# Attention and expert layers on one core: the guess of batch 2 formed ahead of its attention, units 0 and 1 summed on VectorE

## The chip, the cores and the metric

The kernel runs on one core of a Trainium2 chip. The metric is the device time of one execution in microseconds; the time of a version is the median of its runs. All times in this text are microseconds unless ns is written.

## The reference

The program takes 8 batches. Each goes through grouped-query attention (16 query heads, 4 key heads, 384 positions, head size 64), and the result, 384 tokens of width 1024 per batch, goes through a two-stage gate with 16 experts (4 groups of 4):

```python
scores = (1 / sqrt(64)) * q @ k.T            # per head, k and v repeated 4 times
attn = exp(scores - max) / sum               # softmax over the 384 keys
x = (attn @ v), heads joined -> (3072, 1024)

g_idx = argmax(x @ w_group, 1)               # one of 4 groups
e_idx = argmax(x @ w_expert[g_idx], 1)       # one of 4 experts in it
weight = softmax value of the group * softmax value of the expert
out = weight * relu(x @ w1[g, e]) @ w2[g, e]
```

## The kernel before, in words

**Attention.** A batch is worked in 24 *units*: 4 key heads by 6 blocks of 64 keys. For unit u, `score` (line 318) multiplies keys and queries on TensorE into a PSUM tile `ps_s` (two take turns), ScalarE takes the exp into a tile `e` (line 324), and `pv` (line 337) multiplies `e` by v into a tile `ps_o`. `Attn.run` issues, for each u, the scores of unit u + 2, then `pv` of unit u, then the lists of steps written for u (`steps1`, `steps2`: a step at 4.5 comes between `pv(4)` and unit 4's tail). So TensorE needs exp u twice: for `pv(u)`, and to free the score tile that unit u + 2 takes.

**Sums of the softmax.** `pair` (line 345) adds the tiles of two units on GpSimd, in place; `reduce` (line 354) sums the result over 32 columns on VectorE and keeps it in `red3`. Units listed in `apart` are not paired: VectorE reduces both tiles by themselves. `lags` says after which unit which reduction is issued. `join_keys` (line 407) adds the parts of a head; it takes one instruction for heads with equally many parts, and one a head otherwise. `sums` (line 416) adds over partitions with TensorE, and two reciprocals (line 432) write `inv`. `normalise` spreads `inv` by a transpose (line 455) and multiplies `xT` by it (line 459, on VectorE, or on GpSimd where told); `cast` (line 464) copies `xT` in bf16 to `xb`, mostly on ScalarE.

**Experts.** All tokens of a batch are first put through one expert. `moe_h` / `ffn_h` (line 636) multiplies `xb` by w1, two column blocks of 128 at a time with 8 parts of the contraction each, `ffn_y` (line 650) multiplies the result by w2, `y_out` (line 669) scales it on ScalarE and stores it. A loop at the end adds further experts where tokens need them.

**The guess.** Which expert a batch is put through is picked from the mean of v, before the attention is done: `vsum` is v summed over the blocks (three adds on GpSimd in `sum_v`, lines 112 to 114; for batch 0 one reduction on VectorE, line 121), `guess_mean` (line 480) multiplies it by a constant into two columns and copies them to `vm` (line 482), `guess_logits` (line 487) multiplies `vm` by the gate's weights, and `pick_guess` (lines 568 to 581) turns that into an index on VectorE. GpSimd reads the index (`read_pick`, line 558) and issues the loads of w1 and w2 (lines 546 and 552). From batch 3 on `pick` does the same with the logits that `gate_softmax` has.

**Order of the work.** Everything is placed by hand; each engine runs its instructions in the order written. Attention 1 (the second) runs with `steps1`, in which the first expert matmuls of batch 0 stand after unit 17. Then `first_block` finishes batch 0's experts, sums batch 1 and begins attention 2 (the third); its steps are `steps2`, with the rest of batch 1's casts, the guess for batch 2 and the gate matmuls of batch 1 (`second_gate`, line 474). `block(b)` for b from 2 on then does the experts of batch b - 1, the sums and `normalise` of batch b, its gate matmuls, and starts attention b + 1. In `block(2)` alone the guess for batch 3 is neither ahead nor left out: its mean stands between the two halves of `ffn_y` for the second row block, its logits behind the gate matmuls. GpSimd and SyncE also issue the loads: v by SyncE, k and q by GpSimd, the transposes of k and q by SyncE.

## Time and profile before

| | us |
|---|---|
| median of 3 runs (lowest, highest) | 357.18 (356.93, 357.27) |
| the profiled execution | 356.70 |
| its span, first to last instruction | 354.9 |
| TensorE busy | 345.9 |
| VectorE busy | 253.9 |
| ScalarE busy | 225.0 |
| GpSimd busy | 220.2 |

The times of single instructions come from the profiled execution, whose span is 1.8 shorter than its own time; the median is 0.48 above that time. Matmuls are pipelined, so a long duration of one says little: what counts is from one start to the next. Granted clock of TensorE over the span: 0.996 of full speed.

### The profile page before, as it was taken

How to read it: one execution, taken by the hardware profiler on the slowest of the kernel's cores; microseconds unless marked ns; L12 is line 12 of the kernel's file. 1: busy time of each engine (PE TensorE's matmuls, PEld its weight loads, DVE VectorE, ACT ScalarE, POOL GpSimd, SP SyncE). 2: the span in 40 equal slices, each digit the busy share in tenths (PEclk: the TensorE clock that was granted, in tenths of full speed). 3: DMA queues.
4: the chain of work that ended last, by engine and by line, in shares of the span. 5: the costliest groups of instructions: out<-in, count | busy, mean ns of one | idle time of the engine just before them, and what ended most of it. 6: DMA issues, size and time to landing. Idle time of an engine off the chain costs nothing.

```text
span 354.9 us, 9208 instructions
## 1 busy us (share of the span) xinstructions
PE 345.9 (97%) x3801; PEld 182.5 (51%) x3816; DVE 253.9 (72%) x520; ACT 225.0 (63%) x296; POOL 220.2 (62%) x171
## 2 busy tenths in 40 slices
PE   8999999999999999999999999999999999999994
PEld 4455565445555455554555555545545545555642
DVE  5797769767697777976689667886769677796031
ACT  5899925299536795378954499355982669444311
POOL 7889985869935499308991299804995059900000
PEclk9999999999999999999999999999999999999998
DMA  8979999799989999999999999999995995099925
GB/s 199 215 135 188 220 207 160 134 275 222 193 174 176 258 209 182 206 163 203 229 221 207 193 220 211 218 192 193 228 211 95 197 263 130 2 175 219 258 48 137
DMA packets 69327, 67.15 MB, mean 189 GB/s; under 512 B 37113, under 2 KB 49401, under 8 KB 69281
## 3 DMA queue, kind: packets, MB, share of 16 engines
q0 software_dynamic: 26640, 41.03, 67.2%
q1 hardware_dynamic: 42272, 24.94, 30.4%
q8 instruction: 32, 0.52, 0.6%
q10 hardware_dynamic: 368, 0.54, 0.4%
q14 instruction: 15, 0.11, 0.1%
HBM read 86.07 MB, written 12.58 MB: 278 GB/s over the span
## 4 chain that ended last, share of the span: by engine, by line
PE 87%; ACT 4%; POOL 3%; DVE 2%; issue 1%; DMA 1%; ACTq 0%; SPq 0%; POOLq 0%; DVEq 0%
PE ps_o L337 30%; PE ps_s L636 22%; PE ps_s L650 13%; PE ps_s L318 8%; PE ps_o L650 6%; PE ps_o L474 3%; ACT e L324 2%; POOL w L345 2%; PE ps_o L636 1%; PE ps_s L951 1%; PE ps_o L951 1%; DMA w<-in_q_dram 1%; POOL xb L466 1%; ACT w L324 0%; DVE inv L432 0%
## 5 line engine op out<-in xcount | busy, mean ns | idle before, releaser
L345 POOL TENSOR_TENSOR e<-e 128x768 f32<-128x768 f32 x91 | 162.8, 1826 | 37.0 <-PE ps_s L318 30.8
L324 ACT ACTIVATE e<-ps_s 128x768 f32<-128x768 f32 x187 | 147.7, 813 | 15.0 <-PE ps_s L318 12.8
L337 PE MATMUL ps_o<-e,v_raw 64*64 64x384 f32 x1496 | 150.1, 482 | 0.0
L354 DVE TRANSPOSE_TENSOR_REDUCE red<-e 128x24 f32<-128x768 f32 x95 | 91.4, 972 | 36.7 <-POOL e L345 36.6
L636 PE MATMUL ps_s<-xb,w 128*128 128x384 bf16 x480 | 80.1, 326 | 0.1
L337 PEld LDWEIGHTS ps_o<-e,v_raw 64*64 64x64 f32 x1496 | 55.3, 133 | 35.7 <-issue 29.5
L636 PEld LDWEIGHTS <-w 128*128 128x128 bf16 x512 | 49.4, 98 | 36.4 <-issue 4.5
L318 PE MATMUL ps_s<-qT,kT 64*64 64x384 bf16 x768 | 65.0, 325 | 0.4
L650 PEld LDWEIGHTS <-hT 128*128 128x128 bf16 x336 | 31.5, 98 | 37.7 <-issue 1.5
L650 PE MATMUL ps_s<-w,hT 128*128 128x512 bf16 x217 | 49.5, 379 | 0.4
L640 ACT ACTIVATE hT<-ps_s 128x768 bf16<-128x768 f32 x23 | 18.6, 810 | 46.7 <-PE ps_s L636 43.3
L318 PEld LDWEIGHTS <-kT 64*64 64x64 bf16 x768 | 24.5, 105 | 35.6 <-issue 33.6
L669 ACT ACTIVATE ot<-ps_s,we 128x1024 f32<-128x1024 f32 x14 | 15.6, 1115 | 19.0 <-PE ps_s L650 17.2
L604 POOL COPY tok<-qT 1x1 bf16<-1x1 bf16 x6 | 1.1, 179 | 42.5 <-DMA qT<-q_raw 42.5
L379 DVE COPY xT<-ps_o 128x768 f32<-128x768 f32 x26 | 24.0, 924 | 2.7 <-ACT xb L464 1.5
L455 DVE STREAM_TRANSPOSE e<-inv 128x768 f32<-128x768 f32 x26 | 25.2, 971 | 0.2
L464 ACT CAST xb<-xT 128x768 bf16<-128x768 f32 x28 | 23.1, 830 | 3.4 <-DVE xT L459 3.2
L650 PE MATMUL ps_o<-w,hT 128*128 128x512 bf16 x105 | 24.0, 379 | 1.1 <-issue 1.1
L459 DVE TENSOR_TENSOR xT<-xT,e 128x768 f32<-128x768 f32 x24 | 23.1, 962 | 0.8
L495 DVE STREAM_TRANSPOSE gl<-ps_o 128x96 f32<-128x96 f32 x8 | 2.3, 283 | 18.7 <-PE ps_o L474 15.0
L643 ACT ACTIVATE hT<-ps_s 128x384 bf16<-128x384 f32 x14 | 6.1, 488 | 12.5 <-PE ps_o L480 7.2
L474 PEld LDWEIGHTS ps_o<-xT,wg 128*32 128x32 f32 x448 | 9.2, 110 | 3.3 <-issue 2.1
(140 smaller groups left out, 233.3 us busy)
## 6 DMA issues: line engine op xcount, KB each, us to landing
w<-in_moe_w_dram POOLq DMA_DIRECT2D x16, 2048.0 KB, 21.9
out_dram<-ot SPq DMA_DIRECT2D x42, 256.0 KB, 6.9
q_raw<-in_q_dram POOLq DMA_DIRECT2D x7, 768.0 KB, 11.0
v_raw<-in_v_dram SPq DMA_DIRECT2D x7, 384.0 KB, 5.7
k_raw<-in_k_dram POOLq DMA_DIRECT2D x7, 192.0 KB, 6.4
out_dram<-ot SPq DMA_DIRECT2D x10, 128.0 KB, 2.4
w<-in_q_dram POOLq DMA_DIRECT2D x3, 192.0 KB, 6.3
w<-in_k_dram SPq DMA_DIRECT2D x2, 192.0 KB, 3.7
```

Source lines behind the costliest of these rows:

```text
L318: nc.tensor.matmul(out=sT[r * H2:(r + 1) * H2, s, :S], lhsT=kT[b][s * D:(s + 1) * D, key_block(b, s, g // 2, c), ks], rhs=qT[b][s * D:(s + ...
L324: nc.scalar.activation(e.rearrange("p t (s x) -> p s t x", s=2), sT[:, :, :S].rearrange("p s (t x) -> p s t x", t=2), ACT.Exp, scale=scale)
L337: nc.tensor.matmul(out=oT[t * D:(t + 1) * D, r, :S], lhsT=vraw[b][r * H2:(r + 1) * H2, g // 2, c * D:(c + 1) * D], rhs=self.e[u][r * H2:(r ...
L345: nc.gpsimd.tensor_add(out=self.e[u - 1], in0=self.e[u - 1], in1=self.e[u])
L354: nc.vector.tensor_reduce(out=red3[b][:, g, parts[b][g]].rearrange("p t j -> p (t j)"), in_=self.e[w].rearrange("p t (j x) -> p (t j) x", ...
L379: nc.vector.tensor_copy(out=dst, in_=src)
L455: nc.vector.transpose(out=rb.rearrange("p k (j x) -> p k j x", x=32), in_=inv[b][:, ks].unsqueeze(3).to_broadcast([P, 2, NB, 32]))
L459: eng.tensor_mul(out=x, in0=x, in1=rb)
L464: nc.scalar.copy(out=xb[b][:, ks, :], in_=xT[b][:, ks, :])
L474: nc.tensor.matmul(out=pt[32 * t:32 * t + 32, 0, :S // 4], lhsT=wg[:, head_pair(m), :], rhs=x[:, t], start=(m == 0), stop=(m == KQ - 1))
L636: nc.tensor.matmul(out=h[:, jj, :S], lhsT=w1[:, head_pair(m), (f0 + jj) * P:(f0 + jj + 1) * P], rhs=x[:, m, :], start=(m == 0), stop=(m == ...
L650: nc.tensor.matmul(out=y[:, nh, :], lhsT=hT[:, f, c * P:(c + 1) * P], rhs=w2[:, f, nh * HALF:(nh + 1) * HALF], start=(f == 0), stop=(f == ...
```

## The change

- The v of batch 2 is summed by one reduction on VectorE in the steps after unit 17 of the second attention, not by three adds on GpSimd in `first_block`.
- The product for the guess of batch 2 stands behind the sums of batch 1 in `first_block`, in columns 192 and 193 of the same PSUM tile, and `vm` is copied behind the reciprocals. The logits and the pick stand after unit 1 of the third attention (before: the mean after unit 1, logits and pick after unit 2).
- In the third attention units 0 and 1 are not paired on GpSimd: VectorE reduces both after unit 2. Head 0 then has four parts and the others three, so head 0 is joined apart, after unit 10.
- The three casts of batch 1 that stood after units 1, 3 and 6 stand together at 4.5, behind the gate matmuls.
- In `block(2)` the mean of the guess for batch 3 comes behind the gate matmuls, and its logits behind the first scores of attention 3.
- `ffn_h` with f0 = 0 (in every batch) takes the first 6 parts of the contraction for both column blocks, then the last 2 parts.

```diff
--- before.py
+++ after.py
@@ -115,12 +115,12 @@
                              in1=s[:, :, 2 * D:])
         vsum[b] = t
 
-    def first_sum_v():
-        vsum[0] = gpool.tile([P, NA * D], BF16, name="vsum")
+    def reduce_v(b):
+        vsum[b] = gpool.tile([P, NA * D], BF16, name="vsum")
         with nc.allow_low_precision(reason="the guess of an expert alone reads this"):
             nc.vector.tensor_reduce(
-                out=vsum[0].rearrange("p (a d) -> p a d", d=D),
-                in_=vraw[0].rearrange("p a (c d) -> p a d c", d=D), axis=AX.X, op=ALU.add)
+                out=vsum[b].rearrange("p (a d) -> p a d", d=D),
+                in_=vraw[b].rearrange("p a (c d) -> p a d c", d=D), axis=AX.X, op=ALU.add)
 
     def new_qT(b):
         qT[b] = xpool.tile([P, KQ * SC, P], BF16, name="qT")
@@ -409,8 +409,9 @@
                 in_=red3[b][:, g:h, :parts[b][g]].rearrange("p g c t j -> p g (t j) c"),
                 axis=AX.X, op=ALU.add)
 
-    def sums(b, g0, g1, which, tiles=False):
-        sm = ps_tile(which)[:, :, :(g1 - g0) * 2 * NB]
+    def sums(b, g0, g1, which, tiles=False, mean=None):
+        pt = ps_tile(which)
+        sm = pt[:, :, :(g1 - g0) * 2 * NB]
         for r in range(2):
             if not tiles:
                 nc.tensor.matmul(out=sm[:, r], lhsT=half32[:, r, :],
@@ -423,6 +424,8 @@
                     out=sm[t * D:(t + 1) * D, r].rearrange("p (g t j) -> p g t j", t=2, j=NB)[:, :, t],
                     lhsT=half32[rs, r, t * D:(t + 1) * D], rhs=red[b][rs, g0:g1, t],
                     start=True, stop=True)
+        if mean is not None:
+            guess_product(mean, pt, MEAN)
         if b not in inv:
             inv[b] = gpool.tile([P, KQ, NB], F32, name="inv", bufs=2)
         iv = inv[b][:, 2 * g0:2 * g1].rearrange("p (g r) j -> p r g j", r=2)
@@ -430,6 +433,7 @@
         for t in range(2):
             ts = slice(t * D, (t + 1) * D)
             nc.vector.reciprocal(out=iv[ts], in_=sm[ts, :, :, t])
+        return pt if mean is None else guess_copy(pt, MEAN)
 
     Q = P // 4
 
@@ -475,12 +479,19 @@
                                  lhsT=wg[:, head_pair(m), :], rhs=x[:, t],
                                  start=(m == 0), stop=(m == KQ - 1))
 
+    MEAN = 2 * KQ * NB
+
+    def guess_product(b, pt, n):
+        nc.tensor.matmul(out=pt[:, 1, n:n + 2], lhsT=vsum[b], rhs=halfb, start=True, stop=True)
+
+    def guess_copy(pt, n):
+        vm = gpool.tile([P, 2], BF16, name="vm")
+        nc.vector.tensor_copy(out=vm, in_=pt[:, 1, n:n + 2])
+        return vm
+
     def guess_mean(b, pt):
-        pm = pt[:, 1, :2]
-        nc.tensor.matmul(out=pm, lhsT=vsum[b], rhs=halfb, start=True, stop=True)
-        vm = gpool.tile([P, 2], BF16, name="vm")
-        nc.vector.tensor_copy(out=vm, in_=pm)
-        return vm
+        guess_product(b, pt, 0)
+        return guess_copy(pt, 0)
 
     def guess_logits(vm, out_):
         for r in range(2):
@@ -631,11 +642,13 @@
 
     def ffn_h(x, w1, hT, f0, which):
         h = ps_tile(which)
-        for jj in range(2):
-            for m in range(KQ):
-                nc.tensor.matmul(out=h[:, jj, :S],
-                                 lhsT=w1[:, head_pair(m), (f0 + jj) * P:(f0 + jj + 1) * P],
-                                 rhs=x[:, m, :], start=(m == 0), stop=(m == KQ - 1))
+        ends = [0, KQ] if f0 else [0, KQ - 2, KQ]
+        for m0, m1 in zip(ends, ends[1:]):
+            for jj in range(2):
+                for m in range(m0, m1):
+                    nc.tensor.matmul(out=h[:, jj, :S],
+                                     lhsT=w1[:, head_pair(m), (f0 + jj) * P:(f0 + jj + 1) * P],
+                                     rhs=x[:, m, :], start=(m == 0), stop=(m == KQ - 1))
         if f0 + 2 < FQ:
             nc.scalar.activation(hT[:, f0:f0 + 2, :], h[:, :, :S], ACT.Relu)
         else:
@@ -730,7 +743,7 @@
     index_constants()
     steps0 = {
         0: [gate_matrix_2],
-        2: [do(first_q1, "x"), first_sum_v],
+        2: [do(first_q1, "x"), do(reduce_v, 0)],
         4: [do(first_k, NC, 2 * NC, "x")],
         7: [do(x_mean, 0)],
         8: [do(x_logits, 0)],
@@ -780,6 +793,7 @@
             lambda: mean(1, state["pt"]),
             do(at[1].pair, 7),
             do(at[1].reduce, 7),
+            do(reduce_v, 2),
             do(moe_h, 0, 2, "s"),
             do(at[1].pair, 13),
             do(at[1].pair, 15),
@@ -799,13 +813,12 @@
     def first_block():
         load_v(3)
         moe_y(0, 0, "s")
-        sum_v(2)
         load_k(3)
         load_q(3)
         at[1].reduce(NU - 1)
         join_keys(1, 0, Hkv)
         y = ffn_y(w2s[0], hTs[0], 1, "s", (0,))
-        sums(1, 0, Hkv, "o")
+        state["vm"] = sums(1, 0, Hkv, "o", mean=2)
         ffn_y(w2s[0], hTs[0], 1, "s", (1,), y)
         y_out(0, 1, y)
         y = ps_tile("o")
@@ -813,7 +826,7 @@
         normalise(1, 2, "x")
         cast(1, 0)
         ffn_y(w2s[0], hTs[0], 2, "o", (0,), y)
-        at[2] = Attn(2, later=(1,), lags={5: [1], 6: [3], **{u: [u - 2] for u in range(7, NU, 2)}})
+        at[2] = Attn(2, apart=(1,), lags={6: [3], **{u: [u - 2] for u in range(7, NU, 2)}})
         at[2].score(0)
         at[2].score(1)
         ffn_y(w2s[0], hTs[0], 2, "o", (1,), y)
@@ -821,6 +834,10 @@
         normalise(1, 1, None, pool)
         normalise(1, 3, None, pool)
 
+    def second_logits():
+        state["pt"] = ps_tile("x")
+        x_logits(2)
+
     def second_gate():
         gate_logits(1, state["pt"])
         state["gl"] = gate_rows(state["pt"], False)
@@ -828,12 +845,11 @@
     first_block()
     before_attention(2)
     steps2 = {
-        1: [do(cast, 1, 2), do(at[2].pair, 1), do(x_mean, 2)],
-        2: [do(x_logits, 2)],
-        3: [do(cast, 1, 1)],
-        4.5: [second_gate],
-        6: [do(cast, 1, 3)],
+        1: [second_logits],
+        2: [do(at[2].reduce, 1)],
+        4.5: [second_gate, do(cast, 1, 2), do(cast, 1, 1), do(cast, 1, 3)],
         8: [do(read_pick, 2)],
+        10: [do(join_keys, 2, 0, 1)],
     }
     at[2].run(steps2)
 
@@ -865,7 +881,7 @@
             pick_w2(b)
         moe_h(f, 0, "s")
         at[b].reduce(NU - 1)
-        join_keys(b, 0, Hkv)
+        join_keys(b, int(b == 2), Hkv)
         if b == 2:
             gate_softmax(1, state["gl"], False)()
             out_weights(1)
@@ -893,16 +909,16 @@
         y = ffn_y(w2s[f], hTs[f], 1, "s", (0,))
         if ahead:
             guess_logits(vm, guess_out(pt))
-        elif not last:
-            vm = guess_mean(b + 1, pt)
         ffn_y(w2s[f], hTs[f], 1, "s", (1,), y)
         y_out(f, 1, y)
         gate_logits(b, pt)
         if not (last or ahead):
-            guess_logits(vm, guess_out(pt))
+            vm = guess_mean(b + 1, pt)
         if b <= EARLY:
             at[b + 1] = Attn(b + 1)
             at[b + 1].start()
+        if not (last or ahead):
+            guess_logits(vm, guess_out(pt))
         cast(b, 3)
         w = gate_softmax(b, gate_rows(pt, not last), not last)
         if not last:
```

Three engines show how the order moves. First ScalarE, from the second exp of the third attention on (`e` are the exps, `ot` the output scaling of batch 0's third row block, `xb` the casts of batch 1). Before:

```order
L324 ACTIVATE e<-ps_s_1158 128x2x2x192
L669 ACTIVATE ot<-ps_o_1134,we 128x1024
L324 ACTIVATE e<-ps_s_1188 128x2x2x192
L324 ACTIVATE e<-ps_s_1200 128x2x2x192
L464 CAST xb<-xT 128x768
L324 ACTIVATE e<-ps_s_1217 128x2x2x192
L324 ACTIVATE e<-ps_s_1243 128x2x2x192
L464 CAST xb<-xT 128x768
L324 ACTIVATE e<-ps_s_1256 128x2x2x192
L324 ACTIVATE e<-ps_s_1301 128x2x2x192
```

and with the change:

```order
L324 ACTIVATE e<-ps_s_1158 128x2x2x192
L682 ACTIVATE ot<-ps_o_1134,we 128x1024
L324 ACTIVATE e<-ps_s_1188 128x2x2x192
L324 ACTIVATE e<-ps_s_1200 128x2x2x192
L324 ACTIVATE e<-ps_s_1227 128x2x2x192
L324 ACTIVATE e<-ps_s_1241 128x2x2x192
L324 ACTIVATE e<-ps_s_1253 128x2x2x192
L468 CAST xb<-xT 128x768 x3
L324 ACTIVATE e<-ps_s_1301 128x2x2x192
```

The casts that stood behind exps 3, 5 and 8 now stand in a row behind exp 6.

Next GpSimd in `first_block`, from the weight loads of batch 1's expert on. Before:

```order
L552 DMA w_1068<-in_moe_w_dram 128x8x1024
L112 TENSOR_TENSOR vs<-v_raw 128x384
L113 TENSOR_TENSOR vs<-vs 128x2x64
L114 TENSOR_TENSOR vsum<-vs 128x128
L96 DMA k_raw<-in_k_dram 128x2x384
L101 DMA q_raw<-in_q_dram 128x8x384
L459 TENSOR_TENSOR xT<-xT,e 128x768 x2
```

and with the change:

```order
L563 DMA w_1070<-in_moe_w_dram 128x8x1024
L96 DMA k_raw<-in_k_dram 128x2x384
L101 DMA q_raw<-in_q_dram 128x8x384
L463 TENSOR_TENSOR xT<-xT,e 128x768 x2
L345 TENSOR_TENSOR e<-e 128x768 x3
```

The three adds on v are gone, so the loads of k and q of batch 3 follow the weights at once; behind the two multiplies come eleven pair sums (three and eight) where there were twelve.

Last VectorE, from the joins of batch 1 into the third attention. Before:

```order
L407 TENSOR_REDUCE red<-red_842 128x24 x4
L432 RECIPROCAL inv<-ps_o_1116 64x2x4x12 x2
L455 STREAM_TRANSPOSE ps_o_1136<-inv 128x2x384
L459 TENSOR_TENSOR xT<-xT,ps_o_1136 128x768
L455 STREAM_TRANSPOSE ps_o_1139<-inv 128x2x384
L459 TENSOR_TENSOR xT<-xT,ps_o_1139 128x768
L455 STREAM_TRANSPOSE e<-inv 128x768 x2
L482 CAST vm<-ps_o_1213 128x2
L568 TENSOR_REDUCE km<-ps_o_1213 128x1
```

and with the change:

```order
L407 TENSOR_REDUCE red<-red_842 128x24 x4
L435 RECIPROCAL inv<-ps_o_1113 64x2x4x12 x2
L489 CAST vm<-ps_o_1113 128x2
L459 STREAM_TRANSPOSE ps_o_1136<-inv 128x2x384
L463 TENSOR_TENSOR xT<-xT,ps_o_1136 128x768
L459 STREAM_TRANSPOSE ps_o_1139<-inv 128x2x384
L463 TENSOR_TENSOR xT<-xT,ps_o_1139 128x768
L459 STREAM_TRANSPOSE e<-inv 128x768 x2
L579 TENSOR_REDUCE km<-ps_o_1211 128x1
```

The copy of `vm` moved from behind the last transposes up to behind the reciprocals. Further down the two reductions of units 0 and 1 come behind the pick and ahead of the transpose of the gate's logits:

```order
L592 TENSOR_SCALAR oh_all<-ps_o_1211 128x16
L354 TENSOR_REDUCE red_1238<-e 128x24 x2
L506 STREAM_TRANSPOSE gl<-ps_o_1211 128x96
L379 COPY xT<-ps_o_1195 128x768
L354 TENSOR_REDUCE red_1238<-e 128x24 x3
L407 TENSOR_REDUCE red<-red_1238 128x24
L354 TENSOR_REDUCE red_1238<-e 128x24
```

Before, one reduction stood behind that transpose in place of the two ahead of it, and there was no join of one head:

```order
L581 TENSOR_SCALAR oh_all<-ps_o_1213 128x16
L495 STREAM_TRANSPOSE gl<-ps_o_1213 128x96
L354 TENSOR_REDUCE red_1313<-e 128x24
L379 COPY xT<-ps_o_1195 128x768
L354 TENSOR_REDUCE red_1313<-e 128x24 x4
```

## Rows read from the trace of the kernel before

**Rows 1.** The page, part 4: the chain that ended last, share of the span by engine.
```profile
PE 87%; ACT 4%; POOL 3%; DVE 2%; issue 1%; DMA 1%; ACTq 0%; SPq 0%; POOLq 0%; DVEq 0%
```

**Rows 2.** Timeline of TensorE, 43.2 to 47 us: start us, us, engine, line, operation, tiles, count.
```profile
44.29 3.01 PE L636 MATMUL ps_s<-xb,w 128*128 128x384 bf16 x16
```

**Rows 3.** Chain of waits, 30 to 100 us: start us, us, what.
```profile
44.66 0.82 POOL xb L466
...
45.52 1.78 PE ps_s L636 x10
...
66.90 0.43 PE ps_o L416 x4
...
68.11 0.77 DVE inv L432
...
77.95 0.16 DVE oh_all L581
```

**Rows 4.** Timeline of TensorE, 72.9 to 83.5 us (the third attention).
```profile
78.16 1.53 PE L474 MATMUL ps_o<-xT,wg 128*32 128x96 f32 x64
79.61 0.36 PE L318 MATMUL ps_s<-qT,kT 64*64 64x384 bf16 x4
...
82.06 0.33 PE L318 MATMUL ps_s<-qT,kT 64*64 64x384 bf16 x4
...
83.12 0.36 PE L318 MATMUL ps_s<-qT,kT 64*64 64x384 bf16 x4
```

**Rows 5.** Timeline of GpSimd, 60 to 100 us.
```profile
66.94 0.45 POOL L113 TENSOR_TENSOR vs<-vs 128x128 f32<-128x128 f32 x1
...
77.43 21.41 POOL L345 TENSOR_TENSOR e<-e 128x768 f32<-128x768 f32 x12
```

**Rows 6.** Timeline of all engines, 95.2 to 101 us (block 2).
```profile
95.04 5.37 PE L636 MATMUL ps_s<-xb,w 128*128 128x384 bf16 x32
...
99.89 0.48 DVE L407 TENSOR_REDUCE red<-red 128x96 f32<-128x288 f32 x1
...
100.94 0.33 PE L636 MATMUL ps_s<-xb,w 128*128 128x384 bf16 x1
```

**Rows 7.** Chain of waits, 95 to 118 us.
```profile
101.11 5.20 PE ps_s L636 x32
...
113.24 1.46 PE ps_o L474 x64
...
115.29 0.16 issue
```

**Rows 8.** Line 121: engine, operation, tiles, count: ns min/median/max, first and last start us.
```profile
L121 DVE TENSOR_REDUCE vsum<-v_raw x1: 1519/1519/1519, 11.3 to 11.3; 128x128 bf16<-128x768 f32 x1
```

**Rows 9.** Timeline of VectorE, 48.5 to 51.8 us (idle before, and who ended it).
```profile
48.91 0.16 DVE L482 CAST vm<-ps_o 128x2 bf16<-128x2 f32 x1 [1.73 <-PE ps_o L480]
48.99 0.97 DVE L354 TRANSPOSE_TENSOR_REDUCE red<-e 128x24 f32<-128x768 f32 x1
51.57 0.28 DVE L495 STREAM_TRANSPOSE gl<-ps_o 128x96 f32<-128x96 f32 x1 [1.62 <-PE ps_o L487]
```

**Rows 10.** Timeline of ScalarE, 68 to 84 us.
```profile
73.09 1.11 ACT L669 ACTIVATE ot<-ps_o,we 128x1024 f32<-128x1024 f32 x1
74.10 1.50 ACT L324 ACTIVATE e<-ps_s 128x768 f32<-128x768 f32 x2
75.48 0.84 ACT L464 CAST xb<-xT 128x768 bf16<-128x768 f32 x1
76.20 1.53 ACT L324 ACTIVATE e<-ps_s 128x768 f32<-128x768 f32 x2
```

**Rows 11.** Timeline of VectorE, 105 to 113 us (block 2).
```profile
112.63 0.16 DVE L482 CAST vm<-ps_o 128x2 bf16<-128x2 f32 x1
```

**Rows 12.** Timeline of VectorE, 66.6 to 73.1 us (after the second attention).
```profile
67.35 1.52 DVE L432 RECIPROCAL inv<-ps_o 64x96 f32<-64x96 f32 x2 [1.64 <-PE ps_o L416]
```

**Rows 13.** Timeline of GpSimd, 106 to 110 us (block 2).
```profile
107.89 1.26 POOL L113 TENSOR_TENSOR vs<-vs 128x128 f32<-128x128 f32 x1
```

## The prediction

> **What bounds the kernel now.** I read the page's chain of waits first: 87% of it is TensorE [rows 1], so the time is the length of TensorE's queue plus the places where that queue stands still. A wait between other engines that TensorE does not share costs nothing. From the end of the third attention (95.1 us) on I found one stall of TensorE in the chain; the others lie between 44 and 83 us. So I read the chain for 30 to 100 us and the timelines of single engines there.
>
> The reader should see four places. (1) The first expert matmuls of batch 0 (line 636) begin at 44.29 [rows 2]. Six of the sixteen run; the other ten start only at 45.52, when GpSimd's last cast ends at 45.48 [rows 3]. (2) In the third attention a unit costs TensorE 0.82 us where nothing waits: three of them from 79.61 to 82.06 [rows 4]. Unit 9 comes 1.06 after unit 8 (83.12), behind an exp that stood behind a cast on ScalarE. (3) The gate matmuls of batch 1 (line 474) start at 78.16, and the last operation of the guess on VectorE ended at 78.11 [rows 3, 4]: they wait for the guess. (4) GpSimd's twelve pair sums run without a gap from 77.43 to 98.84 [rows 5]. The join behind them ends at 100.37, and TensorE, done with 32 matmuls from 95.04, needs that join for the sums of batch 2 [rows 6].
>
> **The change part by part.** Times are on the old clock of the profiled execution.
>
> *First expert matmuls, split 6 and 2 (ffn_h with f0 = 0).* Thirty-two such matmuls take 5.20 us [rows 7], so 0.1625 each. Six from 44.29 end at 45.27; the seventh starts at 45.52. With the change twelve come ahead of the part that needs the cast and end at 46.24, after the cast. The stall of 45.52 - 45.27 = 0.25, taken as **-0.24**, goes. The split adds no instruction; in the later blocks the casts are done long before, and it changes nothing.
>
> *Sum of v for batch 2 on VectorE.* One reduction: the same form ran once, in 1519 ns [rows 8]. It enters behind the reduction that ends at 49.96, in an idle stretch of 1.62 us that ends at 51.57 with TensorE's matmuls for the guess [rows 9]. It ends at 51.48; those matmuls come 0.24 earlier than before, so VectorE's gate chain starts 0.1 earlier than before instead of 0.24. The sums of batch 1 that hang on that chain have more room than this (third rival). So **0**, hidden. GpSimd's three adds go, and the loads of k and q of batch 3 are issued some 2 us earlier, behind the same two weight loads in the same queue; I give that nothing.
>
> *Product for the guess beside the sums of batch 1, cast of vm behind the reciprocals.* The product is a matmul more here and one less in the attention. The cast of 0.16 lies in the chain of reciprocals, transpose, multiply and ScalarE's first cast, ahead of the output scaling at 73.09 [rows 10]. Two rows bound it. Behind a vm cast at 48.91 the next instruction began at 48.99, before the cast had ended: 0.08 [rows 9]. The second reciprocal, which moves from partitions 0-63 to 64-127, began at 68.11 and took 0.77 [rows 3], half of the 1.52 that both took from 67.35 [rows 12]: no overlap. The vm cast comes behind that second one and goes back to partition 0, so I take the whole 0.16; the ends are 0 and 0.2. The Trainium skill, VectorE: DVE Perf Modes, section Two Vector instructions with no wait between them, has this as a rule: an instruction that starts in another quadrant of partitions than the last one on that memory is held until all before it have finished. With the row at 48.91 the total below would be -1.22, by the rule it is -1.14.
>
> *The third attention.* On ScalarE two exps back to back take 1.38 (74.10 to 75.48), so 0.69 each, a cast 0.72 (75.48 to 76.20), the output scaling 1.01 (73.09 to 74.10) [rows 10]; an exp's result is there 0.81 after its start. Now three casts stand together behind exp 6. ScalarE with the 0.16: scaling 73.25, exp 2 at 74.26, exps 3 to 6 at 74.95, 75.64, 76.33 and 77.06 (0.04 allowed for TensorE's scores), casts 77.75, 78.47, 79.19, exp 7 at 79.91, ready at 80.72. TensorE: unit 2 waits for exp 2 (ready 75.07) and starts at 75.12, with the guess's two matmuls hidden in that wait; units 3 and 4 at 75.94 and 76.76; the gate matmuls at 77.68 instead of 78.16, since the guess on VectorE now starts a unit earlier and is done by about 77.0. They last 1.45 (78.16 to 79.61 [rows 4]): unit 5 at 79.13, unit 6 at 79.95, unit 7 at 80.77 (exp 7 and TensorE itself arrive within 0.05 of each other), unit 8 at 81.59, unit 9 at 82.41. Before, it was 83.12 [rows 4]: **-0.71**. From there the exps (0.69) outrun the units (0.82), as before. The ends: -0.88 if the vm cast is free and no exp is late, -0.4 if each of the six steps to exp 7 takes 0.05 more.
>
> *Units 0 and 1 summed by VectorE; first group joined apart.* GpSimd loses one sum of 21.41 / 12 = 1.78 [rows 5]. VectorE gains one reduction (0.97 [rows 9]) and a small join, in a stage where it often waits for GpSimd. GpSimd's last sum then ends near 97.1 and the join near 98.6, 1.8 earlier. TensorE's 32 matmuls from 95.04 end at 100.24, the sums take 0.43 where nothing waits (66.90 [rows 3]), so the next matmul should come at 100.67; it came at 100.94 [rows 6]. That wait, **-0.27**, goes. (If GpSimd were not relieved, the 0.95 gained before would all be lost here.) What is late next is VectorE's work up to the gate of batch 2 (first rival).
>
> *Guess for batch 3 moved behind the gate matmuls.* No instruction more; its logits now stand between eight score matmuls and line 650. Nothing in the old trace shows that order. The nearest row is the 0.16 of issue between those scores and line 650 [rows 7]. I take **+0.08**, half of one more such gap; the ends are -0.05 and +0.3 (two gaps). VectorE's gate chain there starts some 0.6 later, and only the next pick and a late output wait for it.
>
> Sum: -0.24 - 0.71 - 0.27 + 0.08 = **-1.14**. The profiled execution took 356.70 (span 354.9), 0.48 under the median of the three runs, so it would take 355.6, and the median is 357.18 - 1.14 = **356.0**. With all ends on the good side it is -1.44 (355.7), on the bad side -0.6 (356.6).
>
> **The rivals.**
>
> *Taken back at the gate of batch 2.* If VectorE's chain after the join does not move, the gate matmuls there cannot start before its last multiply, which ended by 112.63 [rows 11]; they started at 113.24 [rows 7]. Then at most 0.61 of the gain survives: 357.18 - 0.61 + 0.08 = 356.65. For it: the chain is serial, from the join through a softmax, reciprocals and four multiplies. Against: it starts 1.8 earlier when GpSimd does. Chance 0.16.
>
> *The three casts cost what they save.* Three casts in a row are 2.16 of ScalarE; the gate matmuls cover 1.45. If exp 7 comes 0.7 later than I worked out (a cast waiting for GpSimd's multiply, for instance), unit 9 is where it was, and only 0.24 + 0.27 - 0.08 = 0.43 is left: 356.75. For it: exp 7 and TensorE meet within 0.05. Against: GpSimd's multiplies for those casts are done when its pair sums begin, 77.43 [rows 5], before the first cast. Chance 0.13.
>
> *Slower: the new reduction on VectorE is stretched beside GpSimd.* It stands ahead of VectorE's gate chain, which ends in the pick that GpSimd reads ahead of its last four pair sums; behind these come the last reduction, the joins, and the sums of batch 1 at 66.90. A short add of GpSimd shows what stretching can do: 0.45 at 66.94 [rows 5], 1.26 at 107.89 [rows 13], a factor of 2.8. The joins were done 1.64 before the reciprocals at 67.35, at 65.71 [rows 12], and TensorE would come to the sums near 66.6, so it decides from about 0.9 us over 1.52. At 2.8 times 1.52 = 4.25 TensorE would wait 1.85, and the time is 357.18 - 1.14 + 1.85 = 357.9. Against: the 1519 ns [rows 8] are the whole instruction in a stage where GpSimd was summing pairs too. Chance 0.06. The Trainium skill, GPSIMD Engine Reference, section 8 Key points, puts such contention on VectorE instructions with two inputs in SBUF or in a two-port mode; the reduction has one input, and the 1.26 stood beside a multiply with two.
>
> **How the numbers follow.** The forecast has 0.65, the rivals 0.16, 0.13 and 0.06. About 0.2% (0.7 us) is what a measurement of this kernel can tell from no change, so faster means below 356.47. Of the forecast some 0.62 lies there; its bad end and the first two rivals (356.6 to 356.8) are no change, 0.31; the third rival and a little unknown are slower, 0.07. The range holds the forecast's ends and the first two rivals: 355.5 to 356.9.
>
> **What would show it.** In the new profile: no gap after the sixth expert matmul at 45; the reduction of line 121 near 50 lasting 1.5; gate matmuls of batch 1 less than 0.2 after unit 4's end; three casts in a row on ScalarE and unit 7 without a wait over 0.1; eleven pair sums in a row on GpSimd; no wait of the sums of batch 2 for the join. It is wrong if TensorE waits in the third attention as long as before, if the gate of batch 2 waits for VectorE, or if the sums of batch 1 wait for the joins.

## The result, and the profile after

The changed kernel takes **360.31 us** (median of 8 runs, 359.00 to 362.65) where the kernel before takes 357.33 (8 runs, 356.93 to 358.47): ratio 1.0083, 95% interval 1.0054 to 1.0112. It is slower by 3.0 us; the forecast was 356.0, and the range ended at 356.9. The profiled execution took 360.43 (span 358.7).

Up to 135 us nearly everything came as forecast. These rows answer to the four places of the prediction. First the chain of waits of the changed kernel, 30 to 125 us (start us, us, what):

```profile
44.39 2.71 PE ps_s L649 x16
...
67.91 0.76 DVE inv L435
...
68.69 0.17 DVE vm L489
...
68.88 1.00 DVE ps_o L459
...
77.51 1.46 PE ps_o L478 x64
...
99.64 0.42 PE ps_o L417 x4
100.05 5.20 PE ps_s L649 x32
```

The sixteen expert matmuls from 44.39 run in one piece; before, they broke after six [rows 2, 3]. The cast of vm stands whole in the chain at 68.69: the reciprocal ahead of it ends at 68.67, the transpose behind it starts at 68.88, so the cast costs its 0.17 and a little more. The gate matmuls of batch 1 start at 77.51 by this view, where they started at 78.16 [rows 4]. In block 2 the sums are followed at once by the next matmul (99.64 + 0.42 = 100.06); the 0.27 of [rows 6] is gone. VectorE and TensorE by their timelines:

```profile
49.86 1.46 DVE L121 TENSOR_REDUCE vsum<-v_raw 128x128 bf16<-128x768 f32 x1
51.36 0.28 DVE L506 STREAM_TRANSPOSE gl<-ps_o 128x96 f32<-128x96 f32 x1
```

```profile
77.44 1.53 PE L478 MATMUL ps_o<-xT,wg 128*32 128x96 f32 x64
...
79.73 0.33 PE L318 MATMUL ps_s<-qT,kT 64*64 64x384 bf16 x4
...
80.73 0.36 PE L318 MATMUL ps_s<-qT,kT 64*64 64x384 bf16 x4
...
82.35 0.36 PE L318 MATMUL ps_s<-qT,kT 64*64 64x384 bf16 x4
```

and ScalarE, 70 to 84 us (exps 2 to 6, the three casts, exp 7 and on):

```profile
74.03 3.76 ACT L324 ACTIVATE e<-ps_s 128x768 f32<-128x768 f32 x5
77.68 2.29 ACT L468 CAST xb<-xT 128x768 bf16<-128x768 f32 x3
79.87 4.56 ACT L324 ACTIVATE e<-ps_s 128x768 f32<-128x768 f32 x6
```

The reduction for vsum took 1.46 us, not stretched. Unit 9 of the third attention starts at 82.35, where it started at 83.12 [rows 4]. Unit 7 comes at 80.73, next to the 80.77 that I had worked out, but that nearness is luck: 80.77 was on the old clock, without the 0.24 of the split, and with it unit 7 should have come at 80.53. It is 0.20 late, 1.00 behind unit 6 where a unit costs 0.82, so the sign "unit 7 without a wait over 0.1" is not met. ScalarE's exps 2 to 6 took 3.65 (74.03 to 77.68) where I had given them 3.49; with the casts, exp 7 began 0.20 late.

The simplest way to see where time goes is to lay the two traces side by side and follow the start of the same matmul in both, after minus before:

| place | shift, us | step |
|---|---|---|
| behind the first expert matmuls, 47 us | -0.21 | -0.24 |
| unit 9 of the third attention, 83 us | -0.78 | -0.58 |
| behind the sums of batch 2, 101 us | -1.05 | -0.27 |
| first unit of the fourth attention, 119 us | -1.06 | 0 |
| behind the guess product of block 3, 148 us | +2.10 | **+3.15** |
| 24 matmuls later, 154 us | +3.78 | **+1.69** |
| end | +3.78 | 0 |

So the sum of my terms, -1.14, was there as -1.06, and then 4.84 us are lost in one place, in block 3, where the diff changes nothing. The chain of waits of the changed kernel there, 136 to 160 us:

```profile
136.72 2.14 POOL e L345 x2
138.86 7.38 DMA qT<-q_raw
...
146.81 0.89 POOL q_raw L101
...
147.71 1.02 POOL vs L112
...
148.81 1.06 POOL vs L113
...
149.94 0.47 POOL vsum L114
...
150.45 0.18 PE ps_o L485
150.63 6.89 PE ps_s L663 x24
```

and the waits in the same stretch, first of the changed kernel, then of the kernel before (engine, line, waited for: us in total, times, longest):

```profile
POOL q_raw L101 <- DMA qT<-q_raw: 5.0, 1, 5.0
...
PE ps_o L485 <- POOL vsum L114: 3.0, 1, 3.0
...
POOL k_raw L96 <- DMA kT<-k_raw: 0.8, 1, 0.8
```

```profile
POOL q_raw L101 <- DMA qT<-q_raw: 1.5, 1, 1.5
```

GpSimd and TensorE in the kernel before, by their timelines:

```profile
143.54 0.89 POOL L101 DMA_DIRECT2D q_raw<-in_q_dram  x1 [1.50 <-DMA qT<-q_raw]
144.45 1.01 POOL L112 TENSOR_TENSOR vs<-v_raw 128x384 f32<-128x384 f32 x1
145.54 0.47 POOL L113 TENSOR_TENSOR vs<-vs 128x128 f32<-128x128 f32 x1
146.09 0.47 POOL L114 TENSOR_TENSOR vsum<-vs 128x128 bf16<-128x128 f32 x1
```

```profile
148.37 0.17 PE L480 MATMUL ps_o<-halfb,vsum 128*128 128x2 bf16 x1
```

To be read from the bottom: TensorE's product for the guess of batch 4 (line 485, one small matmul) waits 3.0 us for GpSimd's vsum. GpSimd forms it with three adds (147.71 to 150.41), which stand in its queue behind the loads of k(5) and q(5). Load_q may not overwrite q_raw before the DMA transposes of q(4) have read it, and these were issued at 138.86 and landed 7.38 us later; GpSimd waited 5.0 us for them, before 1.5. In the kernel before vsum was there at 146.56 and TensorE came at 148.4: 1.8 us to spare, so nothing showed. Now TensorE comes 1.06 earlier and vsum 3.85 later.

The last row of the chain holds the other 1.69: 24 matmuls took 6.89 us, 5.21 before (148.53 to 153.74). The window table of the changed kernel gives the granted clock (window, its length, busy time and count of PE, PEld, DVE, ACT and POOL, then PEclk, DMA share, GB/s):

```profile
147.40:150.50 3.10, 0.12 (x3) 0.05 (x3) 2.12 (x2) 2.42 (x4) 2.82 (x4) 1.00 0.87 178
150.50:157.60 7.10, 7.10 (x28) 2.90 (x29) 3.85 (x5) 1.77 (x2) 0.00 (x0) 0.76 1.31 150
```

TensorE worked 0.12 of the 3.10 us of waiting, and got a mean clock of 0.76 in the 7.1 us behind it; 151.5 to 153.0 us shows 0.50, the lower level of 1.2 GHz. On the page the slice of PEclk there is an 8 between slices of 9.

Why is vsum 3.85 later? 0.58 of it is GpSimd's second add (line 113), which took 1.06 here and 0.47 before; no run shows why. The other 3.27 is load_q, issued at 146.81 instead of 143.54. The loads form a chain of their own on GpSimd and the DMA queues: transposes of q(3) land, a small copy on GpSimd that waits for them (tok, line 615) lets the weight loads of batch 2 go, behind these k and q of batch 4 are loaded, then transposed, then load_q(5) may go, then the sum. This chain does not contain TensorE, so it did not get shorter by 1.06. It got longer, at two places: the transposes of q(3) took 7.2 us instead of 5.5, those of q(4) 7.4 instead of 5.6. The DMA views around the former, first of the kernel before, then of the changed kernel:

```profile
qT<-q_raw SPq DMA_TRANSPOSE x1, 5.5
```

```profile
q8 instruction: 1, 0.02, 0.8%
q14 instruction: 1, 0.01, 0.2%
...
qT<-q_raw SPq DMA_TRANSPOSE x1, 7.2
```

### The profile page after: what moved, and what is told of

Same layout as the page of the kernel before. It is cut to its first block, busy times and chain, and to the rows that moved or that the text cites. A ratio compares the mean times of both kernels' runs of the same rounds, so it can differ in the third digit from the quotient of the medians.

```text
span 358.7 us, 9221 instructions
## 1 busy us (share of the span) xinstructions
PE 348.5 (97%) x3816; PEld 183.3 (51%) x3816; DVE 257.2 (72%) x523; ACT 225.0 (63%) x296; POOL 216.3 (60%) x167
## 4 chain that ended last, share of the span: by engine, by line
PE 89%; DMA 3%; ACT 3%; POOL 2%; DVE 1%; issue 1%; ACTq 0%; SPq 0%; POOLq 0%; DVEq 0%
PE ps_o L337 33%; PE ps_s L649 19%; PE ps_s L663 14%; PE ps_s L318 9%; PE ps_o L663 6%; PE ps_o L478 3%; DMA qT<-q_raw 2%; ACT e L324 2%; PE ps_o L649 1%; PE ps_s L967 1%; PE ps_o L967 1%; DMA w<-in_q_dram 1%; POOL e L345 1%; ACT w L324 0%; DVE inv L435 0%
## 5 line engine op out<-in xcount | busy, mean ns | idle before, releaser
L345 POOL TENSOR_TENSOR e<-e 128x768 f32<-128x768 f32 x90 | 161.0, 1826 | 34.8 <-PE ps_s L318 31.4
L354 DVE TRANSPOSE_TENSOR_REDUCE red<-e 128x24 f32<-128x768 f32 x96 | 92.4, 972 | 36.0 <-POOL e L345 35.7
L663 PE MATMUL ps_s<-w,hT 128*128 128x512 bf16 x224 | 51.5, 388 | 0.0
L663 PE MATMUL ps_o<-w,hT 128*128 128x512 bf16 x112 | 25.5, 380 | 0.0
L463 DVE TENSOR_TENSOR xT<-xT,e 128x768 f32<-128x768 f32 x24 | 24.2, 1008 | 0.8
```

The lines of the kernel that those rows point to most:

```text
L345: nc.gpsimd.tensor_add(out=self.e[u - 1], in0=self.e[u - 1], in1=self.e[u])
L354: nc.vector.tensor_reduce(out=red3[b][:, g, parts[b][g]].rearrange("p t j -> p (t j)"), in_=self.e[w].rearrange("p t (j x) -> p (t j) x", ...
L463: eng.tensor_mul(out=x, in0=x, in1=rb)
L663: nc.tensor.matmul(out=y[:, nh, :], lhsT=hT[:, f, c * P:(c + 1) * P], rhs=w2[:, f, nh * HALF:(nh + 1) * HALF], start=(f == 0), stop=(f == ...
```

## The experiments

Theory 1: the change gains its 1.06 us, and the loss is TensorE's wait for GpSimd's sum in block 3 with the slow clock behind it. Theory 2: some part of the change costs the time by itself. Theory 3: the late transposes cost it whatever stands behind them. With a time I give the ratio to the kernel before, run beside it, and the 95% interval. A caution for single traces: some profiled executions, one of the changed kernel too, are up to 1 us late within the first 20 us already; I take shifts from behind that point.

### Where the sum stands, and the parts alone

The sum ahead of the loads, in the changed kernel (e1) and in the kernel before (e2):

```diff
+            if not last:
+                sum_v(b + 1)
             if b + 2 < B:
                 load_k(b + 2)
                 load_q(b + 2)
-            if not last:
-                sum_v(b + 1)
```

> The changed kernel with one more edit: in the blocks from batch 3 on, GpSimd forms the tile sum for the next guess before it issues the loads of k and q, not behind them. Theory 1 (the loss is TensorE's wait for GpSimd's vsum in block 3, because that sum stands behind load_q, which waits until the transposes of q have read q_raw): vsum is there at about 143 us, TensorE arrives at 147.4 and waits for nothing, the 3.0 us of wait and the 1.7 us of slow clock behind it go, and the gain of 1.06 us that the trace shows up to 135 us reaches the end: 356.2 us, 1.1 under the kernel before. The transposes of q may still take 7.2 us. Theory 2 (a part of the change costs the time itself, by more traffic or a slower clock): the time stays at 360. Theory 3 (late transposes are the cause whatever stands behind them: the loads of the later batches come late too): the wait moves to the next user of these loads and 358 to 360 us are left.

Measured: 358.60 us (12 runs, 357.16 to 363.46), ratio 1.0030 (1.0005 to 1.0055). The wait for vsum and the slow clock are gone and TensorE keeps 1.06 us up to 180 us, as theory 1 says. But it does not reach the end, and the time is in the range of theory 3, though the transposes of q(4) took 5.51 here: in blocks 4 and 5 of the profiled run it loses 0.63, 0.65 and 0.68 at matmuls that start at 191.28, 223.51 and 234.62, each right behind the landing of a weight load (191.23, 223.46, 234.58). The waits there, of which the one put down to ScalarE is the third of these:

```profile
PE ps_s L649 <- DMA w<-in_moe_w_dram: 0.6, 1, 0.6
PE ps_s L663 <- ACT hT L656: 0.5, 1, 0.5
PE ps_s L663 <- DMA w<-in_moe_w_dram: 0.5, 1, 0.5
```

> The kernel before with the same move of GpSimd's sum ahead of the loads from batch 3 on, nothing else. Theory 1: no wait is there to be taken away (vsum is ready at 146.6 us, TensorE comes at about 148.5), so the time stays within 0.3 us of 357.3. Theory 2 says nothing else. Theory 3: loads of k(5) and q(5) are issued up to 1.8 us later, so up to +0.5 us if a later guess hangs on them.

Measured: 358.25 (12 runs), 1.0039 (1.0023 to 1.0054): slower, which theory 1 in its simple form had not said. In its trace the load of k(5) is asked for at 144.0 instead of 141.3 us, since the sum stands ahead. The profiled run (358.23) keeps step with the kernel before up to 245 us and then loses 0.95, in the seventh attention and block 6. There the transposes of q(7) land at 247.45 instead of 240.34, GpSimd stands at the copy that waits for them, its pair sums begin at 249.85 instead of 246.11, and TensorE waits for copies of outputs behind them. So even the kernel before cannot have its loads 2 us later for nothing; theory 3 has a part in it.

Next the parts alone: the split of ffn_h on the kernel before (e3), and the changed kernel with ffn_h in one pass (e4):

```diff
+        ends = [0, KQ] if f0 else [0, KQ - 2, KQ]
+        for m0, m1 in zip(ends, ends[1:]):
```

> The kernel before with only the first pair of ffn_h of each batch split in two passes over its depth. Theory 1: TensorE runs 0.2 us ahead, which leaves 1.7 us of the 1.9 us that vsum is early in block 3, so the 0.2 us reach the end: 357.1 us, unless the transposes of q of batches 3 and 4 take 7.2 us in place of 5.5, in which case vsum is 1.5 to 3 us later and part of a wait is back. Theory 2 (the split itself costs, for it is in every batch): slower than 357.3 by 0.5 us or more, the same in each batch.

Measured: 357.46, ratio 1.0001 (0.9991 to 1.0011). That is not the 357.1 of theory 1, and no cost of the split either. In its profiled run, the slowest of the 12 (358.74), the 0.24 us are there up to block 3; the transposes of q(4) took 7.06, vsum came at the moment at which TensorE did (0.08 lost), and TensorE then waited for the weights of batch 3 at 180 and 191 us (+0.92 and +0.61). The gain of the split does not reach the end.

> The changed kernel with ffn_h in one pass as before; the guess, the pair summed on VectorE and the first group joined apart all stay. Theory 1: TensorE is 0.85 us ahead in block 3; with transposes of q of 5.5 us nothing waits and it takes 356.5 us, with two of 7.2 us it waits 2.8 us and then loses 1.7 to the clock: 360. So the time must go with the wait of that product for vsum in its own trace. Theory 2 (guess part costs the time): 360.3 and no such wait in block 3.

Measured: 360.84 (359.19 to 361.48), 1.0090 (1.0071 to 1.0110). Transposes of q(3) and q(4) of 7.2 and 7.3 us, a step of +2.79 at the product in block 3 and +1.46 behind it: theory 1's second case.

### The changed kernel once more

> The changed kernel once more, for a second profile. Theory 1: the same wait of TensorE for vsum in block 3, 2.5 to 3.5 us, with a granted clock under 1 behind it, and the transposes of q of batches 3 and 4 at 7.1 to 7.4 us each. If it is chance that they were slow, one of them takes 5.5 us here, and the wait is shorter by 1.6 us.

Measured: one run, 363.11 us. Both transposes slow again (7.18 and 7.53), the step at the product 0.55 larger than in the first profile, and that behind it 2.75 instead of 1.69: after the wait 22 matmuls took 7.28 us. The start of this run was 1.0 late. These three make up the 2.6 us between the two profiles; the other runs of the changed kernel have no trace.

### Giving the chain room, one place at a time

E5 fetches the weights of batch 3 ahead of the loads of batch 5 (in block 3: sum, copy, weights, load_k, load_q). `EARLY` is the first block that loads k and q ahead of the weights:

```diff
         if not early:
+            if b > 2:
+                sum_v(b + 1)
             after_transposes(b + 1)
             pick_w1(b)
             pick_w2(b)
-            sum_v(b + 1)
+            if b == 2:
+                sum_v(b + 1)
             load_k(b + 2)
             load_q(b + 2)
...
-    EARLY = 3
+    EARLY = 4
```

> The changed kernel, in whose block 3 GpSimd now forms the tile sum first and then fetches the weights of batch 3 ahead of the loads of k and q of batch 5 (as block 2 does for its own; one block more is treated that way, so the first two units of the fifth attention's successor are scored in block 4 too). Theory 1 with a second bound, which the run with the sum moved first gave (1.05 us ahead up to 180 us, then three waits of 0.63, 0.65 and 0.68 us for weights that land late): the weights of batch 3 land about 12 us earlier, at 176 us against a need at 179 us, so neither the wait for vsum nor those of block 4 are there, and the gain of 1.06 us reaches the end: 356.3 us. If the loads of batch 5, which then come behind the weights, are late in turn, a wait appears for the weights of batch 4 at 222 or 233 us: up to 358. Theory 2 (a part of the change costs the time by itself): 358 to 360.

Measured: 357.33 (12 runs, 355.76 to 360.43), 1.0014 (0.9988 to 1.0039). In the profiled run, at 355.76, TensorE waits for no other engine between 60 and 350 us and ends 0.83 ahead of the kernel before. Half the runs lie between 355.8 and 356.6, half between 358.1 and 360.4: right in the one, the "late in turn" of the expectation fits the other, whose traces I do not have.

E6 and e7 leave out the copy of block 2, in the changed kernel and in the one before:

```diff
         if not early:
-            after_transposes(b + 1)
             pick_w1(b)
```

> The changed kernel without the small copy on GpSimd in block 2 that makes the weight loads of batch 2 wait until the transposes of q of batch 3 have landed; the sum for the guess stays behind load_q in block 3. Theory 1 (the chain transposes, weights, k and q, transposes, load_q, sum sets when vsum is there): the weights are asked for some 10 us earlier, k and q of batch 4 land at about 128 us, their transposes are done before GpSimd comes to load_q at 141 us, vsum is ready at about 144 us against TensorE's 147.4, no wait, 356.3 us. If weights and transposes slow each other, the transposes of batch 3 land later, but nothing needs them before 118 us. Theory 2: 360.

> The kernel before without that same copy in block 2. Theory 1: no wait to take away, 357.3 us within 0.3; if it gets faster by more, the kernel before had waits for these loads in its usual runs that its one trace does not show.

Measured: 371.58, 1.0399 (1.0386 to 1.0413), and 357.90, 1.0015 (1.0007 to 1.0024). The transposes of q(3) took 28.6 us beside the weight loads in the first and 9.5 in the second. "Nothing needs them before 118 us" was wrong: the scores of the next attention do, at 113.7, and TensorE waited 13.1 us for them. E7, for which 357.3 within 0.3 was expected, is a miss too: it is slower, not equal. That copy has to stay in block 2.

E9 puts the sum between the two loads, e10 a second copy ahead of them in block 3:

```diff
             if b + 2 < B:
                 load_k(b + 2)
+            if not last:
+                sum_v(b + 1)
+            if b + 2 < B:
                 load_q(b + 2)
-            if not last:
-                sum_v(b + 1)
```

```diff
+            if b == EARLY:
+                after_transposes(b + 1)
             if b + 2 < B:
                 load_k(b + 2)
```

> The changed kernel with GpSimd's sum between the loads of k and q in the blocks from batch 3 on, so that the load of k(5) is again asked for at 141.1 us, some 2.2 us into the transposes of q(4). Theory 1: vsum is ready at about 143.7 us and no wait for it is left. Theory on the transposes (those of q(4) land 1.7 us late where the load of k(5) is asked for 2.0 to 2.2 us into them, as in three traces, and not where it comes 3.4 us into them or later, as in the traces with the sum first): they take 7.2 us or more here, so load_q comes at about 146.8 and the weights of batch 3 land as in the changed kernel, at 181.2 and 193.2 us, against needs of 179.4 and 189.8: waits of about 1.8 and 1.6 us in block 4 in the place of the one taken away, 359.5 us. If the place of that load does not matter, the transposes take 5.5 us and the time is that with the sum first, 358.6.

Measured: 360.84, 1.0097 (1.0074 to 1.0120). The transposes of q(4) took 7.31 as expected and no wait for vsum was left; but those of q(5) took 7.18 too, and the loss appeared at a place I had not named, in the fifth attention:

```profile
POOL tok L615 <- DMA qT<-q_raw: 17.8, 1, 17.8
DVE red L354 <- POOL e L345: 10.4, 4, 8.0
...
PE ps_o L337 <- DVE xT L379: 3.7, 1, 3.7
```

GpSimd stood at the copy that waits for q(5) until 166.2 us, so its pair sums of the fifth attention began at 168.6; VectorE's reduction waited 8.0 us for the first of them, the copy of an output to SBUF (line 379) stood behind that reduction, and TensorE waited 3.7 us for the copy.

> The changed kernel with its own order on GpSimd (load of k, load of q, sum) in block 3, but the three held until the transposes of q(4) have landed. Theory on the transposes: without the load of k(5) in them they take 5.5 us and land at 144.4 us instead of 146.2; load_q is asked for at 145.2, vsum is ready at 148.8 instead of 150.4, so TensorE waits 1.4 us instead of 3.0 and loses less to the clock behind it: 358 to 359 us, faster than the changed kernel though a wait was added. If that load has nothing to do with it, the transposes take 7.2 us still, vsum comes at 150.7 and the time is 360.5 or more.

Measured: 361.46 (359.55 to 362.88), 1.0117 (1.0088 to 1.0146). Right on the transposes, 5.51 us; wrong on the time. The held loads were issued at 145.95 and 146.69, and the three adds took 3.5 us instead of 2.7, so vsum came at 151.1 and TensorE waited 3.2 us, as long as in the changed kernel. The run is worth having for the clock behind that wait:

```profile
147.80:151.20 3.40, 0.23 (x4) 0.06 (x3) 2.40 (x3) 2.42 (x4) 3.12 (x3) 1.00 1.10 191
151.20:156.60 5.40, 5.40 (x28) 2.47 (x29) 3.85 (x5) 1.77 (x2) 0.00 (x0) 1.00 1.29 144
```

The 24 matmuls took 5.20 us here (a step of +3.34 and none behind it), against 6.89. About the same idle time (2.98 and 3.17 us) cost 1.7 us of clock in one run and nothing in the other.

E11 is e1 with the copy left out in block 3; e12 and e13 are that again, with the first scores of batch 5 moved into block 4, on the changed kernel and on the kernel before:

```diff
                 before_attention(b + 1)
-                after_transposes(b + 2)
+                if b > EARLY:
+                    after_transposes(b + 2)
```

and, in e12 and e13 alone:

```diff
-        if b <= EARLY:
+        if b <= EARLY + 1:
             at[b + 1] = Attn(b + 1)
...
-            elif b + 1 < B:
+            elif EARLY + 1 < b < B - 1:
                 nxt = at[b + 1] = Attn(b + 1)
```

> The changed kernel with the sum ahead of the loads from batch 3 on, and in block 3 alone without the copy that makes the weight loads of batch 3 wait for the transposes of q(5). Theory 1 with the second bound: the weights of batch 3 are asked for at about 146 us, behind the loads of k and q of batch 5 in the queue, and land at about 172 and 184 us, before TensorE needs them at 179.4 and 189.8; the transposes of q(5), which then run beside them, take 20 us and more, but nothing needs them before about 184 us. No wait in blocks 3 and 4: 356.3 us. If those transposes land after 186 us, the loads of batch 6 on GpSimd and with them the weights of batch 4 come late, and a wait at 222 or 233 us takes the gain back: 357 to 359.

Measured: 362.60, 1.0157 (1.0139 to 1.0175). Weights early, as expected; the transposes of q(5) took 26.8 us, and "nothing needs them before about 184 us" was wrong, since the fifth attention ends with scores of the sixth, which need q(5):

```profile
PE ps_s L318 <- DMA qT<-q_raw: 5.0, 1, 5.0
```

> The changed kernel with the sum ahead of the loads, without the copy in block 3 that holds the weights of batch 3 behind the transposes of q(5), and with the first two units of the fifth batch's attention scored in block 4 and not at the end of the attention before it, so that these transposes, which take some 27 us beside the weights, have until about 199 us. Theory 1 (the change itself is worth what the forecast said, and only GpSimd's chain of loads took it back): no wait for vsum, for the weights of batch 3 (there at 169 and 181 us against 179.4 and 189.8), for those transposes (183 us) or for GpSimd's pair sums; the gain of 1.06 us reaches the end but for what the later scores cost, 0 to 0.5 us: 356.2 to 356.8, and 0.8 to 1.2 us under the same edits on the kernel before. Theory 2 (the change costs the time by itself): 358 to 360 and slower than the same edits on the kernel before.

> The same edits on the kernel before. Theory 1: nothing waited there, so 357.3 us plus what the later scores cost, 0 to 0.5 us: 357.3 to 357.8, and 0.8 to 1.2 us over the run above.

Measured: 359.70, 1.0080 (1.0052 to 1.0108), and 357.93, 1.0019 (1.0005 to 1.0033). From 116 us on the first profile is 1.16 ahead of the second, and stays so up to 230 us: nothing waits in blocks 3 and 4. Then the weights of batch 4 are late (0.54) and in the seventh attention a copy of an output behind GpSimd's late pair sums (1.17). By their times alone these two runs are what theory 2 had said, 358 to 360 and slower than the same edits on the kernel before; the traces show a lead that lasts past the change and is lost at the loads of later blocks. The chain had been given room in one block and taken it from the next.

E14 and e15 are e1 with the loads of v moved, to see whether these make the links long:

```diff
-        if b + 2 < B:
+        if b + 2 < B and not early:
             load_v(b + 2)
...
                 before_attention(b + 1)
+                load_v(b + 2)
                 after_transposes(b + 2)
```

and in e15, which has no load of v at the head of block 2 either:

```diff
         moe_y(f, 0, "s")
+        if not early:
+            load_v(b + 2)
```

> The changed kernel with the sum ahead of the loads and, from block 3 on, the load of v of the batch after next put on its queue behind the transposes of q instead of ahead of them. Theory 1 with the second bound: the load of q(5) took 10.0 us beside that of v (5.4 us, 384 KB) in the run with the sum first; without it some 8 us, so the transposes of q(5) land and the weights of batch 3 are asked for 2 us earlier, at 160.2 us on the clock of the kernel before, and land at 178 and 188 us against needs of 179.4 and 189.8: the three waits of 0.63, 0.65 and 0.68 us of that run go, 356.3 to 357.0. If the load of q(5) takes 10 us all the same, 358 to 358.6 as with the sum first.

> The run above with the load of v(4) in block 2 moved too, from right behind the transposes of q(3) to behind the store of the first output rows. If the load of v behind them is what makes the transposes of q(3) land 1.7 us late (7.2 us in every run with the guess moved, 5.5 in every run without), they take 5.5 us here, and the whole chain up to the transposes of q(4) is 1.6 us earlier: 356.2 us with more room, none of its runs over 358. If it is the two code loads that start as these transposes end, they still take 7.2 us, and the time is that of the run above.

Measured: 358.11, 1.0012 (0.9983 to 1.0041), and 359.88, 1.0076 (1.0061 to 1.0090). The first came out in the time of its second case, 358 to 358.6: without v beside it q(5) took 11.5 us to load (10.0 in e1, with v). The second was right that the transposes of q(3) can take 7.1 without v behind them, and wrong on the time, 1.8 over the first; q(5) took 9.1 to load. What makes these links long is not the load of v.

### Room in three blocks at once

E16 is e5 with its order in blocks 3, 4 and 5, e17 the same on the kernel before:

```diff
-    EARLY = 4
+    EARLY = 6
```

> The changed kernel with the order of the run with the weights ahead in blocks 3, 4 and 5 and not in block 3 alone: GpSimd forms the tile sum, fetches the weights of the batch, then loads k and q of the batch after next, and the next attention's first two units are scored in the block. Theory 1: the weights of batches 3, 4 and 5 land 8 us and more before TensorE needs them, and the copy that waits for the transposes comes when these have long landed, so it holds none of GpSimd's pair sums; the link that the run with only block 3 reordered had left (weights of batch 4 at 219.4 and 231.2 us against needs of 221.6 and 232.0) is gone. The gain of 1.06 us reaches the end less 0.1 us for each block whose scores come later: 356.0 to 356.6, and no run in 12 above 358. Theory 2 (the change costs the time by itself): as slow as before or slower.

> The same edits on the kernel before. Theory 1: nothing waited there in its one trace, so it takes 357.2 to 357.7 us, 0.9 to 1.2 us more than the run above: that difference is the change alone. If it gets as fast as the run above, the change is worth nothing and the reordered loads are all.

Measured: **356.39 us** (9 runs, 355.99 to 357.17), ratio 0.9971 (0.9960 to 0.9982); and 357.69 (11 runs, 357.41 to 358.64), 1.0008 (0.9999 to 1.0017). In the first, TensorE shows no wait between 60 and 330 us; its weights of batch 4 landed at 204.2 and 215.9 us, where e5 had 219.4 and 231.2. It gives up 0.12 us in each of three blocks for the scores moved into them. The difference of 1.30 us between the two (0.9 to 1.2 was expected) is the change alone; 1.06 to 1.16 of it is the lead that the side-by-side traces show, the rest lies within the spread of the runs. Theory 2 has fallen, theory 1 holds with the chain as its second bound, and this version is faster than both kernels.

## Why the prediction was wrong

**The terms** held in the main. The split: -0.24 forecast, -0.21 at 47 us. The third attention: -0.71 forecast, -0.58 measured, inside the ends of -0.4 and -0.88, and smaller because exp 7 came 0.20 late. The wait for the join: -0.27, measured -0.27. The moved guess of block 2: -1.05 ahead of it and -1.06 behind it, so 0 for the +0.08 that I took. These two misses have opposite signs, and that the sum was met within 0.08 is in part luck. The reduction on VectorE: hidden, 1.46 us long. For the cast of vm I had the choice between 0.08 by one row and 0.16 by another; the whole cast stands in the chain at 68.69, so the row of the reciprocals [rows 3, 12] was the right one, and with it the rule of the Trainium skill that I had set beside it (VectorE: DVE Perf Modes, Two Vector instructions with no wait between them). The three rivals did not happen: the gate matmuls of batch 2 follow at once, exp 7 came 0.20 late and not the 0.7 of the second rival, and the reduction was not stretched.

**The step that failed** is in the first part: "87% of it is TensorE, so the time is the length of TensorE's queue plus the places where that queue stands still", and with it the look at 30 to 118 us alone. A chain that shows TensorE only says that nothing else came later in that one execution; it does not say by how much the next one came earlier. In block 3 that was 1.8 us: vsum ready at 146.56, wanted at 148.4, both in the trace before and neither on the chain. I took 1.06 of the 1.8 and never asked who else runs there. The margin alone would have covered the 1.06; what used it up is that vsum itself came 3.85 later, and the forecast had no term for that. "A wait between other engines that TensorE does not share costs nothing" was the sentence behind it: GpSimd's wait of 1.5 us for the transposes at 143 us was such a wait, and it was the one that grew to 5.0.

**The term given as nothing** was the second half of the failure. Of the earlier loads of k and q of batch 3 I wrote "I give that nothing". For those loads it was right: they landed at 94.28 and 98.10, before at 93.99 and 98.27. But what hangs on them did not stay: the transposes of q(3) landed at 105.30 instead of 103.80, the weights of batch 2 were asked for 1.5 us later and k and q of batch 4 landed 1.4 later, with 1.8 more from the transposes of q(4). With both transposes as before, vsum would have come at about 146.9 (150.41 - 1.68 - 1.81), ahead of TensorE's 147.3, and nothing would have been lost; this is an estimate from these two traces. That the earlier loads are what made the transposes slow is not shown. No rival of mine had a time for a DMA in it.

**The price of the wait** would also have been short in a prediction that had seen it: 3.0 us of waiting cost 4.7, because of the clock.

What stays open: which event makes the transposes slow, and why GpSimd's second add took 0.58 longer. What the traces of all these runs show is told below; no run isolates it. I also have no trace of the slow half of e5's runs.

## What to carry to other kernels

When a chain of waits shows one engine throughout, look for the work that arrives just before that engine needs it, all along the kernel, and write down how early it is; then ask what the change does to that work's own time. A margin larger than the gain is not enough: here it was 1.8 against 1.06, and the work itself came 3.85 later. Loads on an in-order queue that wait for other transfers form a chain of their own, which does not get shorter when the compute does; give it room before shortening the compute, and at every block, since room given at one place was mostly taken from the next. A small product that needs another engine's sum is a wait worth placing on that engine's queue ahead of anything that waits for a transfer.
